# A new prologue order in a fused attention and MLP kernel: norm statistics ahead of applies, all V tiles and wide w1 outputs in the prologue, a bank plan per output

## The chip, the cores and the metric

The kernel runs on one core of a Trainium2 chip. The metric is device time in microseconds (us), the median of three runs. Times named with an engine come from one profiled execution of the kernel before the change.

## The reference, cut to what matters

```python
xn = layernorm(x)                                  # x: 2048 x 448, bf16
qkv = xn @ wqkv                                    # 16 heads of 28
pq, pk = q @ w_phi, k @ w_phi                      # per head, 28 x 28
phi_q = concat(softmax(pq), softmax(-pq))          # 56 features
phi_k = concat(softmax(pk), softmax(-pk))
kv, z = phi_k^T @ v, sum_s(phi_k)
o = (phi_q @ kv) / (phi_q @ z + 1e-6)
A = o @ wo
h = gelu(layernorm(xn) @ w1)                       # four column groups, moved by 1, -1, 2, -2 tokens
x1 = xn + shift(h) @ w2
B = x1 + gelu(layernorm(x1) @ w3) @ w4             # w3: 448 x 1792
out = x + A + B
```

The second layer norm of `xn` is left to the first one in the kernel; `q` and `k` are never formed, because `w_phi` is folded into their weights.

## The kernel before, in words

The 2048 tokens are 16 tiles of 128. The contraction over 448 features uses four overlapping 128-row pieces, held so that every piece has a lower and an upper half of 64 rows; an output needs seven such halves. A matmul on rows 0-63 and one on rows 64-127 run beside each other when their results lie in different PSUM banks, so the code always issues a lower half of one output next to an upper half of another.

A small recorder (`Recorder`) writes every operation into one list in program order. Each engine then executes its own operations in that order, and waits on semaphores where data or a bank demands it. The order written in `play([...])` is therefore the order of each engine's queue. The eight PSUM banks of 512 fp32 columns are assigned by hand. TensorE appears in the profile as PE, VectorE as DVE, ScalarE as ACT, GpSimd as POOL, and SyncE as SP; SP issues most DMAs, and a DMA queued on SP waits behind the ones before it.

The program has three parts.

1. The prologue (lines 361-846, up to 37.76 us). It loads x, normalises it (`ln1`), transposes it into `xnT`, and computes V (`z_v`), the first MLP product with w1 (`z_h`, `z_w1`, `z_rest`) with its GELU, and the folded weights `wpk` and `wpq` (`fold_pair`). `("s", i)` is the statistics of tile i: two VectorE instructions and then the scale on POOL (`ln_scale`: an add and a power, and a negation if POOL is to apply it). `("a", i)` applies it on VectorE, `("p", i)` on POOL. Tiles 0-7 and 12-15 are transposed on TensorE (`xn_T`) with a copy from PSUM; tiles 8-11 go by a DMA transpose on SP (`xn_Td`). `zip_in` issues the lower half of a new output together with the upper half of the one before it. `EV`, `EW` and `rest_out` empty banks: V by a copy, the w1 outputs by a GELU. Column 384 to 447 of w1 is the rest (`z_rest`); its result is transposed by a DMA (`rest_T`), and `h_shift` moves parts of `hT` by the token shifts with six DMAs.
2. The loop of eight passes (lines 858-886, 37.76 to 74.13 us). A pass computes a pair of k tiles, a pair of q pieces, and a side job: either the w2 product of two token tiles (`w2_pair`, added to `xn` on VectorE by `w2_out`) or the V product of two tiles (12 and 13 in pass 1, 14 and 15 in pass 4). From pass 3 it also adds two tiles to the kv product (`kv_tile`, banks 6 and 7). ScalarE takes exponentials of k and q with both signs; `k_norm` sums and inverts on VectorE and multiplies on POOL. The second norm's statistics follow on VectorE (`w2_norm`), and `g_apply` with the DMA transpose `g_T` makes `gT`.
3. The main part (lines 888-947): w3 with GELU (`a(p)` and `b(p)`, halves of a pair), the attention numerators (`N`), the final sums with w4 and wo (`f`), and the stores.

The change touches the x loads (363-374), `xn_T` (492-501), `zip_in` (545-554), the output makers (556-588), `g_apply` (680), `ln1` (797), the two `play` lists (833-846, 920-924) and the pass loop (856-886).

Of the kernel before, what the change touches and what calls it, by code (L numbers as in the profile page):

```python
# [223 lines left out]
def bass_parallel_sum__linear_kernel_hedgehog__mixer_s_mlp__prompt_kernel(  # L224
# [16 lines left out]
    with es:  # L241
# [128 lines left out]
        R.op("ACT", lambda e: e.preload_act_table_set("gelu_apprx_tanh_and_others"), [], [])  # L370
        load_x(6, 2)
        load_x(4, 2, "ACT")
        load_x(12, 4)
        load_x(8, 4, "ACT")
# [117 lines left out]
        def xn_T(i, b, n=1):  # L492
# [6 lines left out]
            for j in range(n):  # L499
                R.act(xnT[:, :, 128 * (i + j):128 * (i + j) + 128].rearrange("p c (h e) -> p c h e", h=2),  # L500
                      t[:, :, 256 * j:256 * j + 256].rearrange("p h (c e) -> p c h e", c=KC), ACT.Copy)
# [40 lines left out]
        KCS = ((0, 1, 2, 3), (0, 2, 3))  # L542
        tail = [None]

        def zip_in(make):
            prev, n4 = tail[0] if tail[0] else (None, True)
            lo = make(LO, KCS[0] if n4 else (0, 1, 3)) if make else []
            hi = prev(HI, KCS[0] if n4 else KCS[1]) if prev else []
            for k in range(max(len(lo), len(hi))):
                for step in (lo[k:k + 1], hi[k:k + 1]):  # L550
                    for mms in step:
                        for out, l, r, first in mms:
                            R.mm(out, l, r, first, False)
            tail[0] = (make, not n4) if make else None

        def z_v(i, b):
            o = banks[b][:, 0:D]

            def make(rows, kcs):
                lo, hi = rows  # L560
                return [[(o, xnT[lo:hi, kc, 128 * i:128 * i + 128], wv[lo:hi, kc, :], rows == LO and n == 0)]
                        for n, kc in enumerate(kcs)]
            return make

        def z_h(t, bs):
            j = 128 * (t % 4)

            def make(rows, kcs):
                lo, hi = rows
                return [[(banks[b][:, j:j + 128], w1[lo:hi, kc, 128 * m:128 * m + 128],  # L570
                          xnT[lo:hi, kc, 128 * t:128 * t + 128], rows == LO and n == 0 and j == 0)
                         for m, b in enumerate(bs)] for n, kc in enumerate(kcs)]
            return make

        def z_w1(g, m, b):
            def make(rows, kcs):
                lo, hi = rows
                return [[(banks[b], w1[lo:hi, kc, 128 * m:128 * m + 128], xnT[lo:hi, kc, 512 * g:512 * g + 512],
                          rows == LO and n == 0)] for n, kc in enumerate(kcs)]
            return make  # L580

        def z_rest(h, b):
            def make(rows, kcs):
                lo, hi = rows
                return [[(banks[b][:, 64 * j:64 * j + 64],
                          xnT[lo:hi, kc, 1024 * h + 128 * j + 2:1024 * h + 128 * j + 130], w1[lo:hi, kc, REST:D],
                          rows == LO and n == 0 and j == 0) for j in range(8)] for n, kc in enumerate(kcs)]
# [92 lines left out]
        def g_apply(i):  # L680
            ln_apply(pool, halves(g_tok[:, i % 4, :]), lap(xn[:, i, :]), mv2, rs2, i)
# [115 lines left out]
        def ln1(*ops):  # L797
            for op, i, *n in ops:
                if op == "s":
                    ln1_stats(i, *(n or (1, 0)))  # L800
                else:
                    ln1_apply(pool if op == "p" else dve, i)

        fps = {(t, m): fold_pair(t, m, b) for t, m, b in ((1, 0, 3), (1, 2, 0), (0, 0, 3), (0, 2, 0))}
# [7 lines left out]
        def ZV(i):  # L812
            return (zip_in, z_v(i, vb[i]))
# [4 lines left out]
        def ZH(t):  # L818
            return (zip_in, z_h(t, (2, 3, 4)))

        def ZW(g, m):
            return (zip_in, z_w1(g, m, gb[g] + m))

        def EW(g, m, n):
            return (w1_out, g, m, gb[g] + m, n)

        def ZR(h, b):
            return (zip_in, z_rest(h, b))

        vb = {0: 5, 1: 6, 2: 7, 3: 5, 4: 6, 5: 7, 6: 5, 7: 6, 8: 5, 9: 6, 10: 3, 11: 4}  # L830
        gb = (2, 0, 0, 5)
        spin(19, 256)
        play([L(("s", 0), ("s", 1), ("a", 0), ("s", 2), ("a", 1), ("s", 3), ("a", 2), ("s", 4), ("a", 3)),
              (xn_T, 0, 0), (spin, 3, 256), (xn_T, 1, 2), ZV(0), ZV(1), (xn_T, 2, 0), ZH(0),
              L(("s", 5), ("a", 4)), EV(0), ZV(2), (xn_T, 3, 0), ZH(1),
              L(("s", 6), ("a", 5)), EV(1), ZV(3), (xn_T, 4, 0), ZH(2),
              L(("s", 7), ("a", 6)), EV(2), ZV(4), (xn_T, 5, 0), EV(3, "DVE"), ZH(3),
              L(("s", 8, 2, 2), ("a", 7)), EV(4), (xn_T, 6, 0), ZV(5), (xn_T, 7, 0), EW(0, 0, 3), ZV(6), ZV(7), EV(5),
              L(("p", 9), ("a", 8)), (xn_Td, 8), (xn_Td, 9), (phi_blocks,),
              ZW(1, 0), ZW(1, 1), EV(6, "ACT", 2), L(("s", 10, 2, 2), ("p", 11), ("a", 10)), (xn_Td, 10), (xn_Td, 11),  # L840
              (load_wT, 0, (1, 2, 3)), ZW(1, 2), ZR(0, 7), EW(1, 0, 3), ZV(8), (rest_out, 0, 7), ZV(9), ZV(10), EV(8, "ACT", 2),
              L(("s", 12, 2, 2), ("p", 13), ("a", 12), ("s", 14, 2, 2), ("p", 15), ("a", 14)), (late_3,), (load_w2,), (rest_T, 0),
# [135 lines left out]
```

## Time and profile before

| item | value |
|---|---|
| time, median of 3 runs (range) | 182.21 us (182.06 to 182.24) |
| profiled execution, time / span | 182.38 / 180.7 us |
| TensorE granted clock | 0.999 |
| TensorE busy | 170.6 us, 94% of the span |
| VectorE / ScalarE / POOL busy | 109.5 / 81.5 / 96.7 us |
| TensorE busy from 6.73 to 37.76 us | 25.68 of 31.03 us |
| TensorE busy from 37.76 to 74.13 us | 35.88 of 36.37 us |
| DMA moved | 16.00 MB, mean 89 GB/s |

A busy share is a mean over parts with different limits, and TensorE's busy time counts a matmul from issue to its modelled end. In the timeline, a note in brackets such as `[0.80 <-DMA xnT<-xn]` is the idle time of the engine just before the row and what ended it. The chain of waits lists start, length, and the work that the end of the run goes back to.

### The profile page before, as it was taken

How to read it: one execution, taken by the hardware profiler on the slowest of the kernel's cores; microseconds unless marked ns; L12 is line 12 of the kernel's file. 1: busy time of each engine (PE TensorE's matmuls, PEld its weight loads, DVE VectorE, ACT ScalarE, POOL GpSimd, SP SyncE). 2: the span in 40 equal slices, each digit the busy share in tenths (PEclk: the TensorE clock that was granted, in tenths of full speed). 3: DMA queues.
4: the chain of work that ended last, by engine and by line, in shares of the span. 5: the costliest groups of instructions: out<-in, count | busy, mean ns of one | idle time of the engine just before them, and what ended most of it. 6: DMA issues, size and time to landing. Idle time of an engine off the chain costs nothing.

```text
span 180.7 us, 5311 instructions
## 1 busy us (share of the span) xinstructions
PE 170.6 (94%) x2323; PEld 91.2 (50%) x2323; DVE 109.5 (61%) x249; ACT 81.5 (45%) x92; POOL 96.7 (54%) x137
## 2 busy tenths in 40 slices
PE   7988977879899999999999999999999999999993
PEld 5566633644455555455455454554555545555551
DVE  5687642478989979834666983651545517474621
ACT  2356646478777977964822422422224213224000
POOL 4655558000779999993065949562350622722740
PEclk9999999999999999999999999999999999999999
DMA  6991346669940114214011241322623120211331
GB/s 162 357 205 22 62 89 160 90 177 335 252 144 4 33 29 76 87 33 83 8 29 33 58 90 31 83 78 60 78 42 83 37 77 0 80 33 29 83 86 44
DMA packets 34743, 16.00 MB, mean 89 GB/s; under 512 B 26016, under 2 KB 34016, under 8 KB 34720
## 3 DMA queue, kind: packets, MB, share of 16 engines
q1 hardware_dynamic: 32944, 14.23, 34.8%
q10 hardware_dynamic: 1776, 1.43, 2.4%
q8 instruction: 18, 0.29, 0.7%
q14 instruction: 5, 0.04, 0.1%
HBM read 7.14 MB, written 1.84 MB: 50 GB/s over the span
## 4 chain that ended last, share of the span: by engine, by line
PE 78%; DVE 9%; DMA 5%; ACT 3%; POOL 1%; issue 1%; ACTq 1%; DVEq 0%
PE banks L203 78%; DMA xtok<-in_A_x_dram 4%; DVE st L215 4%; DVE xn L215 2%; DMA xnT<-xn 1%; ACT hT L211 1%; DVE mv L215 1%; DVE ksum L215 1%; DVE vaug L215 1%; POOL rs L215 1%; ACTq L221 1%; ACT xnT L211 1%; ACT vaug L211 1%; ACT gT L211 0%; DVE rks L215 0%
## 5 line engine op out<-in xcount | busy, mean ns | idle before, releaser
L211 ACT ACTIVATE phik<-banks 128x1024 bf16<-128x1024 f32 (+1 forms) x44 | 42.3, 984 | 63.0 <-PE banks L203 62.9
L203 PE MATMUL banks<-gT,w 64*128 64x512 bf16 x392 | 50.0, 377 | 0.0
L215 DVE TENSOR_TENSOR vaug<-banks,vaug 128x464 f32<-128x464 f32 (+3 forms) x65 | 32.6, 512 | 23.0 <-PE banks L203 21.3
L203 PE MATMUL banks<-w,phik 64*128 64x448 bf16 (+1 forms) x420 | 45.0, 350 | 0.0
L215 POOL TENSOR_TENSOR xnT<-vaug 128x196 bf16<-128x196 f32 (+1 forms) x32 | 18.1, 585 | 46.4 <-DVE vaug L215 46.4
L203 PE MATMUL banks<-wv,xnT 64*128 64x448 bf16 (+1 forms) x218 | 31.8, 350 | 1.2 <-DMA xnT<-xn 1.2
L203 PEld LDWEIGHTS banks<-w,phik 64*128 64x128 bf16 (+1 forms) x420 | 21.7, 94 | 21.2 <-issue 0.4
L215 POOL TENSOR_TENSOR phik<-phik,rks 128x1792 bf16<-128x1792 bf16 x8 | 25.7, 3211 | 10.9 <-DVE rks L215 10.9
L203 PEld LDWEIGHTS banks<-gT,w 64*128 64x128 bf16 x392 | 17.7, 94 | 17.8 <-ACT phik L211 0.4
L203 PEld LDWEIGHTS banks<-wv,xnT 64*128 64x128 bf16 (+1 forms) x218 | 12.1, 94 | 12.2 <-DMA xnT<-xn 2.0
L203 PE MATMUL banks<-xnT,w 64*128 64x128 bf16 (+1 forms) x147 | 16.4, 286 | 0.0
L215 POOL TENSOR_TENSOR vaug<-xn,xtok 128x448 f32<-128x448 bf16 x16 | 16.2, 1032 | 0.2 <-DVE vaug L215 0.2
L215 DVE TENSOR_REDUCE ksum<-phik 128x64 f32<-128x1792 bf16 x8 | 16.1, 2006 | 0.0
L215 DVE RECIPROCAL vaug<-banks 128x16 f32<-128x16 f32 x16 | 4.1, 258 | 17.9 <-PE banks L203 17.9
L203 PE MATMUL banks<-xnT,wpq 64*128 64x512 bf16 x112 | 14.7, 377 | 0.0
L203 PE MATMUL banks<-wpk,xnT 64*128 64x448 bf16 x112 | 13.2, 349 | 1.0 <-ACT gT L211 1.0
L215 DVE TENSOR_TENSOR xn<-banks,xn 128x512 bf16<-128x512 f32 (+1 forms) x16 | 9.2, 616 | 5.6 <-PE banks L203 5.6
L215 POOL TENSOR_SCALAR g_tok<-xn,rs 128x512 bf16<-128x512 bf16 x16 | 12.1, 766 | 0.2
L203 PE MATMUL banks<-w,hT 64*128 64x448 bf16 x96 | 11.7, 350 | 0.5 <-DVE vaug L215 0.5
L215 POOL TENSOR_TENSOR rs<-mv,mhalf 128x1 f32<-128x1 f32 (+2 forms) x16 | 11.3, 705 | 1.3
L215 DVE BATCH_NORM_STATS2 st<-xtok 128x6 f32<-128x448 bf16 x16 | 9.8, 613 | 1.9 <-DMA xtok<-in_A_x_dram 1.9
L211 ACT ACTIVATE xnT<-banks 128x512 bf16<-128x512 bf16 x12 | 6.9, 596 | 7.2 <-PE banks L207 7.2
(66 smaller groups left out, 165.6 us busy)
## 6 DMA issues: line engine op xcount, KB each, us to landing
w<-in_B_w_dram SPq DMA_DIRECT2D x2, 896.0 KB, 6.3
out_dram<-vaug SPq DMA_DIRECT2D x15, 112.0 KB, 1.9
w<-in_B_w_dram SPq DMA_DIRECT2D x1, 1568.0 KB, 10.2
xtok<-in_A_x_dram SPq DMA_DIRECT2D x1, 448.0 KB, 8.2
xtok<-in_A_x_dram ACTq DMA_DIRECT2D x1, 448.0 KB, 8.4
wv<-in_A_wo_dram SPq DMA_DIRECT2D x2, 224.0 KB, 3.9
w<-in_B_w_dram SPq DMA_DIRECT2D x1, 336.0 KB, 3.5
gT<-g_tok SPq DMA_TRANSPOSE x16, 2.5
```

The costliest lines, as they stand in the source:

```text
L203: self.op("PE", lambda e: e.matmul(out, lhsT, rhs, start=start, stop=stop, skip_group_check=True), [out], [lhsT, rhs], tile=self._tile(lhsT))
L211: self.op("ACT", lambda e: e.activation(out, in_, func, **kw), [out], [in_] + aps)
L215: self.op(eng, lambda e: getattr(e, name)(out, *args, **kw), [out], aps)
L221: self.op(eng, lambda e: e.dma_start(out, in_), [out], [in_], dma=True)
```

## The change

Seven things change together.

- x tiles 4 and 5 are loaded one by one on SP's and ScalarE's queues, and the loads of 8-11 and 12-15 keep their queues behind them.
- In the norm, the statistics of tiles 10-11 stand before the applies of 8 and 9, those of 12-13 before 10 and 11, those of 14-15 before 12 and 13.
- `zip_in` merges the two lists of matmuls by columns issued instead of step by step, and takes a list `then`, which is played when the output is whole, that is after the next output's zip.
- w1 group 0 is computed like the other groups, with 512 columns for each of three outputs, in place of four times 128 columns. GELUs take one or two banks instead of three.
- V tiles 12 to 15 are computed at the end of the prologue; the pass loop has w2 jobs in passes 0, 1, 2, 4, 5 and 6 and none in 3 and 7. In passes without a side job the kv tiles come after the first q half.
- Banks are listed per output (`vb`, `gb`) and per pass (`at`: k pair, w2 pair, q pair, each number a pair of banks). The copies of tiles 14 and 15 from PSUM, and the eviction of V4 and V5, go to VectorE; that of V3 goes to ScalarE.
- The second norm's statistics move to fixed passes (`norms`). `g_apply` of tiles 0-3 runs after pass 3; that of tiles 4-7 on VectorE in the main part, after the w2 sum of tile 12, where POOL did it. The kv tiles 14 and 15 come one w3 half later; the load of w3 moves from the middle of the prologue behind `h_shift(1)`.

```diff
         R.op("ACT", lambda e: e.preload_act_table_set("gelu_apprx_tanh_and_others"), [], [])
+        load_x(4, 1)
+        load_x(5, 1, "ACT")
         load_x(6, 2)
-        load_x(4, 2, "ACT")
+        load_x(8, 4, "ACT")
         load_x(12, 4)
-        load_x(8, 4, "ACT")
...
-        def xn_T(i, b, n=1):
+        def xn_T(i, b, n=1, eng="ACT"):
...
+                if eng == "ACT":
+                    R.act(d, a, ACT.Copy)
+                else:
+                    R.ew(dve, "tensor_copy", d, a)
...
+        upper = [[], (), True]
+
+        def zip_in(make, then):
+            high, done, four = upper
+            low = make(LO, (0, 1, 2, 3) if four else (0, 1, 3)) if make else []
+            n, at = [low, high], [0, 200]
+            while n[0] or n[1]:
+                k = int(not n[0] or bool(n[1]) and at[1] < at[0])
+                out, l, r, first = n[k].pop(0)
+                R.mm(out, l, r, first, False)
+                at[k] += max(64, out.shape[-1])
+            play(done)
+            upper[:] = (make(HI, (0, 2, 3) if four else (0, 1, 2, 3)), then, not four) if make else ([], (), True)
...
-        def g_apply(i):
-            ln_apply(pool, halves(g_tok[:, i % 4, :]), lap(xn[:, i, :]), mv2, rs2, i)
+        def g_apply(i, eng=pool):
+            ln_apply(eng, halves(g_tok[:, i % 4, :]), lap(xn[:, i, :]), mv2, rs2, i)
...
-        fps = {(t, m): fold_pair(t, m, b) for t, m, b in ((1, 0, 3), (1, 2, 0), (0, 0, 3), (0, 2, 0))}
+        fps = {(t, m): fold_pair(t, m, b) for t, m, b in ((1, 0, 2), (1, 2, 0), (0, 0, 0), (0, 2, 0))}
...
-        vb = {0: 5, 1: 6, 2: 7, 3: 5, 4: 6, 5: 7, 6: 5, 7: 6, 8: 5, 9: 6, 10: 3, 11: 4}
-        gb = (2, 0, 0, 5)
+        vb = {0: 5, 1: 6, 2: 7, 3: 5, 4: 6, 5: 7, 6: 2, 7: 3, 8: 6, 9: 7, 10: 2, 11: 3, 12: 6, 13: 7, 14: 2, 15: 3}
+        gb = ((2, 3, 4), (0, 1, 4), (4, 6, 7), (5, 2, 3))
         spin(19, 256)
         play([L(("s", 0), ("s", 1), ("a", 0), ("s", 2), ("a", 1), ("s", 3), ("a", 2), ("s", 4), ("a", 3)),
-              (xn_T, 0, 0), (spin, 3, 256), (xn_T, 1, 2), ZV(0), ZV(1), (xn_T, 2, 0), ZH(0),
-              L(("s", 5), ("a", 4)), EV(0), ZV(2), (xn_T, 3, 0), ZH(1),
-              L(("s", 6), ("a", 5)), EV(1), ZV(3), (xn_T, 4, 0), ZH(2),
-              L(("s", 7), ("a", 6)), EV(2), ZV(4), (xn_T, 5, 0), EV(3, "DVE"), ZH(3),
-              L(("s", 8, 2, 2), ("a", 7)), EV(4), (xn_T, 6, 0), ZV(5), (xn_T, 7, 0), EW(0, 0, 3), ZV(6), ZV(7), EV(5),
-              L(("p", 9), ("a", 8)), (xn_Td, 8), (xn_Td, 9), (phi_blocks,),
-              ZW(1, 0), ZW(1, 1), EV(6, "ACT", 2), L(("s", 10, 2, 2), ("p", 11), ("a", 10)), (xn_Td, 10), (xn_Td, 11),
-              (load_wT, 0, (1, 2, 3)), ZW(1, 2), ZR(0, 7), EW(1, 0, 3), ZV(8), (rest_out, 0, 7), ZV(9), ZV(10), EV(8, "ACT", 2),
-              L(("s", 12, 2, 2), ("p", 13), ("a", 12), ("s", 14, 2, 2), ("p", 15), ("a", 14)), (late_3,), (load_w2,), (rest_T, 0),
-              (h_shift, 0), (load_lap, w3, B_w3), ZV(11), ZW(2, 0), EV(10, "ACT", 2), (xn_T, 12, 6, 2), ZW(2, 1), (xn_T, 14, 6, 2), ZW(2, 2),
-              FO(1, 0, 0), FO(1, 0, 1), ZW(3, 0), EW(2, 0, 3), ZW(3, 1), FO(1, 2, 0), FO(1, 2, 1), ZW(3, 2), FO(0, 0, 0),
-              ZR(1, 2), EW(3, 0, 3), FO(0, 0, 1), FO(0, 2, 0), (zip_in, None), (rest_out, 1, 2), FO(0, 2, 1),
-              (rest_T, 1), (h_shift, 1), (load_w4,)])
+              (xn_T, 0, 0), (spin, 3, 256), (xn_T, 1, 2), ZV(0, EV(0)), (xn_T, 2, 0), ZV(1), (xn_T, 3, 2), ZV(2, EV(1)), ZV(3, EV(2)),
+              L(("s", 5), ("a", 4)), (xn_T, 4, 0), ZW(0, 0, EV(3)),
+              L(("s", 6), ("a", 5)), ZW(0, 1), (xn_T, 5, 0), ZW(0, 2, EW(0, 0, 2)),
+              L(("s", 7), ("a", 6)), ZV(4), (xn_T, 6, 0), EW(0, 2, 1),
+              L(("s", 8, 2, 2), ("a", 7)), ZV(5), (xn_T, 7, 0), L(("s", 10, 2, 2), ("p", 9), ("a", 8), (phi_blocks,)), (xn_Td, 8), (xn_Td, 9),
+              ZV(6, EV(4, "DVE", 2)), L(("s", 12, 2, 2), ("p", 11), ("a", 10)), ZV(7), (xn_Td, 10), (xn_Td, 11),
+              ZW(1, 0, EV(6, "ACT", 2)), ZW(1, 1, EW(1, 0, 2)), L(("s", 14, 2, 2)), ZW(1, 2, EW(1, 2, 1)), FO(1, 0, 0), (load_wT, 0, (1, 2, 3)),
+              ZV(8), FO(1, 0, 1), L(("p", 13), ("a", 12), ("p", 15), ("a", 14)), (late_3,), (load_w2,),
+              ZV(9, EV(8, "ACT", 2)), ZR(0, 5, (rest_out, 0, 5), (rest_T, 0), (h_shift, 0)), ZV(10), (xn_T, 12, 0, 2, "ACT"), ZV(11, EV(10, "ACT", 2)),
+              ZW(2, 0), (xn_T, 14, 0, 2, "DVE"), ZW(2, 1), ZW(2, 2, EW(2, 0, 1), EW(2, 1, 2)), FO(1, 2, 0),
+              ZW(3, 0, EW(3, 0, 1)), FO(1, 2, 1), ZW(3, 1), ZW(3, 2, EW(3, 1, 2)), FO(0, 0, 0),
+              ZR(1, 4, (rest_out, 1, 4)), FO(0, 0, 1), ZV(12), ZV(13, EV(12, "ACT", 2)), ZV(14), FO(0, 2, 0),
+              ZV(15, EV(14, "ACT", 2)), FO(0, 2, 1), (zip_in, None, ()),
+              (rest_T, 1), (h_shift, 1), (load_lap, w3, B_w3), (load_w4,)])
...
-        side = [("w", 0), ("v", 12), ("w", 2), ("w", 4), ("v", 14), ("w", 6), ("w", 8), ("w", 10)]
-        g_at = {2: (0,), 3: (1,), 4: (2, 3), 6: (4,), 7: (5,)}
+        side = {0: 0, 1: 2, 2: 4, 4: 6, 5: 8, 6: 10}
+        g_at = {3: (0, 1, 2, 3)}
+        norms = {1: (0, 1), 3: (2, 3), 5: (4,), 6: (5,), 7: (6, 7)}
+        at = {0: (2, 3, 0), 1: (1, 2, 3), 2: (0, 2, 1), 3: (0, None, 2), 4: (1, 0, 2), 5: (1, 0, 2), 6: (1, 0, 2), 7: (1, None, 0)}
         for ps in range(8):
-            k, q = k_pair(2 * ps, 1), q_pair(ps // 2, 2 * (ps % 2), 0)
-            kind, i = side[ps]
-            w = {"w": w2_pair, "v": v_pair}[kind](i, 2)
+            kb, wb, qb = at[ps]
+            k, q = k_pair(2 * ps, kb), q_pair(ps // 2, 2 * (ps % 2), qb)
+            i = side.get(ps)
+            w = w2_pair(i, wb) if i is not None else None
+            kv = [2 * ps - 6, 2 * ps - 5] if ps > 2 else []
             k[0]()
-            if ps > 2:
-                kv_tile(2 * ps - 6)
-                kv_tile(2 * ps - 5)
-            w[0]()
+            if w:
+                for t in kv:
+                    kv_tile(t)
+                w[0]()
             k[1]()
             for s in range(2):
-                k_exp(2 * ps, 1, s)
+                k_exp(2 * ps, kb, s)
             q[0]()
-            w[1]()
-            if kind == "w":
-                w2_out(i, 2)
-            if kind == "v":
-                v_out(i, 4, "DVE" if i == 12 else "ACT")
+            if w:
+                w[1]()
+                w2_out(i, wb)
+            else:
+                for t in kv:
+                    kv_tile(t)
             q[1]()
             for s in range(2):
-                q_exp(2 * ps, 0, s)
-            k_norm(2 * ps)
-            if kind == "w" and i < 8:
-                w2_norm(i)
+                q_exp(2 * ps, qb, s)
+            if ps < 7:
+                k_norm(2 * ps)
+            for j in norms.get(ps, ()):
+                ln_stats(st2, mv2, xn, j)
+                if j % 4 == 3:
+                    ln_scale(mv2, rs2, j - 3, 4, 4)
+            if ps == 7:
+                k_norm(14)
...
-            A(6, 7), G(6, 7),
-            a(0), (wl[12][0],), b(0), a(1), (w2_last, 12), b(1), K(10, 11, 12, 13),
-            a(2), (wl[14][0],), b(2), a(3), K(14, 15), b(3), (kv_copy,),
-            a(4), (w2_last, 14), b(4), a(5), (kv_blocks,), b(5),
+            a(0), (wl[12][0],), b(0), a(1), (w2_last, 12), (lambda: [g_apply(i, dve) for i in (4, 5, 6, 7)],), G(4, 5, 6, 7), b(1), K(10, 11, 12, 13),
+            a(2), (wl[14][0],), b(2), a(3), b(3), a(4), K(14, 15), (kv_copy,), (w2_last, 14), b(4), a(5), (kv_blocks,), b(5),
```

## The prediction

> **What bounds the kernel now.** I read first the 40 slices, then the chain of waits, then the timeline with its idle notes.
>
> ```profile
> PE   7988977879899999999999999999999999999993
> ```
>
> ```profile
> 2.77 6.78 DMA xtok<-in_A_x_dram
> ...
> 16.56 0.71 POOL rs L215
> ...
> 17.58 0.41 DVE xn L215
> ...
> 22.82 2.47 DMA xnT<-xn
> ...
> 37.11 0.60 ACT gT L211
> ...
> 47.62 130.29 PE banks L203 x1706
> ```
>
> The chain has two parts. From 47.62 us on nothing but TensorE work stands in it. Before that it hops between the x load, VectorE's norm chain, POOL's `rs` power, the DMA transposes and ScalarE. So two questions decide: how much TensorE work leaves the late part, and whether the early part takes it in without ending later. The boundary that I use is 37.76, where the first k pair starts. The idle notes name the early waits of TensorE:
>
> ```profile
> 10.78 0.29 PE L207 MATMUL banks<-ident,xn 64*128 64x64 bf16 x8 [0.76 <-DVE xn L215]
> 16.48 0.29 PE L207 MATMUL banks<-ident,xn 64*128 64x64 bf16 x8 [0.59 <-DVE xn L215]
> 24.04 0.93 PE L203 MATMUL banks<-wv,xnT 64*128 64x448 bf16 x8 [0.80 <-DMA xnT<-xn]
> 25.34 0.74 PE L203 MATMUL banks<-wv,xnT 64*128 64x448 bf16 x6 [0.37 <-DMA xnT<-xn]
> 29.14 0.41 PE L207 MATMUL banks<-ident,xn 64*128 64x64 bf16 x16 [1.20 <-ACT xnT L211]
> 33.16 0.68 PE L203 MATMUL banks<-g_tok,hi 64*128 64x84 bf16 x15 [0.48 <-ACT hT L211]
> 37.76 0.93 PE L203 MATMUL banks<-wpk,xnT 64*128 64x448 bf16 x8 [1.02 <-ACT gT L211]
> ```
>
> These are 5.2 us of waits; TensorE is busy 25.68 of the 31.03 us from 6.73 to 37.76, so 5.35 in all. A middle pass (period 60.26 to 64.90, 4.6 us) reads:
>
> ```profile
> 60.26 0.92 PE L203 MATMUL banks<-wpk,xnT 64*128 64x448 bf16 x8
> ...
> 63.00 1.73 ACT L211 ACTIVATE phik<-banks 128x896 bf16<-128x896 f32 x2 [0.24 <-PE banks L203]
> ...
> 64.90 0.92 PE L203 MATMUL banks<-wpk,xnT 64*128 64x448 bf16 x8
> 65.11 1.94 ACT L211 ACTIVATE hi<-banks 128x1024 bf16<-128x1024 f32 x2 [0.38 <-PE banks L203]
> ```
>
> ScalarE has 1.73 + 1.94 = 3.67 us of exponentials in each pass, so TensorE is the bound there, by 0.9 us only.
>
> **The change, part by part.** Unit prices: two 64-row matmuls on different banks run side by side; 14 of 448 columns cost 7 steps. From 8.43, 8.62, 8.81 to 9.00 steps of 448 columns are 0.19 us apart; those of 512 (26.14, 26.37, 26.59) 0.22. An output takes 3.5 steps: 0.67 or 0.76.
>
> *Middle passes.* V12-13 and V14-15 leave passes 1 and 4: 2 x 7 x 0.19 = 2.66 us of TensorE. The 0.49 us wait at 47.62 for V12's eviction goes too. Passes start at 37.76, 41.93, 46.22, 51.04 and so on to 74.13, in all 36.37. After, passes 0 to 2 have a w2 pair and no kv: 3 x 4.17 = 12.5. Passes 4 to 6 keep w2 and kv: 3 x 4.61 = 13.8. Passes 3 and 7 have kv alone: 4.61 - 1.33 = 3.28 each, under ScalarE's 3.67. What is late next? VectorE in pass 1 has the w2 sum 1.16, the k sums 2.01 + 0.55 and two norms 1.5, in all 5.2 against 4.17, so the pass 2 sum comes about 1.2 late and pass 3's q pair, which takes its banks, waits some 0.45. After pass 7 the next pair needs the bank of pass 7's k, whose exponentials end 0.55 later, as ScalarE lags by that. Total 12.5 + 3.7 + 13.8 + 3.3 + 0.55 = 33.9, that is 2.5 less. Bounds: 3.15 less without either stall (2.66 + 0.49), and 0.9 less if both short passes stay at 4.61.
>
> *Norms 4 to 7 of the second layer* go from POOL (0.77 each) to VectorE (4 x 0.41), after the w2 sum of 12. They delay nothing on the path: their transposes issue some 6 us after the pass loop and are read at step a(7), 17 us after it. k_norm(14) now stands behind two norms (1.5 us) on VectorE; its POOL product (3.21) ends some 7.5 us into the main part and the kv tiles 14, 15 now come after a(4), at 11.5. Cost nothing; 4 us of cover, beyond which each us late is a us.
>
> POOL's 0.90 us normalisations at 21.22, 24.48 and 27.75 ran beside VectorE's without a stretch; one at 17.64 took 1.12. The Trainium skill, Advanced Engine Details and Errata, section VectorE Performance Modes, speaks against this move: VectorE's two-port modes and GpSimd block each other on a shared SBUF port. By the rows the POOL product loses nothing; by the rule up to 4 x 0.41 = 1.6 us, still inside the cover.
>
> *Prologue work.* V12-15 add 4 x 0.67 = 2.7 us. w1 group 0 was 4 tiles x 21 matmuls of 128 columns, zipped beside V steps, so 4 x 0.67 = 2.7; it becomes 21 of 512 columns, 3 x 0.76 = 2.3. Net +2.3. The last V15 half runs alone: +0.3.
>
> *x loads.* Tile 4 landed at 9.55 in a 224 KB load on ScalarE's queue, behind w1 (7.6). Now it is a 112 KB load on SP, whose w1 landed at 7.8; the next 224 KB there took 0.8. So about 8.3; bounds 7.9 and 9.55. Tile 3's apply, queued behind tile 4's statistics on VectorE, moves with it: 10.34 becomes 9.1, and TensorE's transpose of tile 3 from 10.78 to 9.5. One more issue on SP (0.45 us) delays tiles 12-15, phi and the weight transposes; all have over 5 us to spare.
>
> *Norm order.* VectorE waited four times for POOL's `rs`, 5.3 us. Statistics of 10-11 now come before the apply of 8, so these waits go. But POOL's apply of 9 falls behind the scale of 10-11, and of 11 behind that of 12-13. My walk on VectorE, with statistics 0.73 and an apply 0.41: from 8.3 each tile takes 1.13, a6 ends at 12.8, the statistics of 8-9 and a7 at 14.6, those of 10-11 at 16.0, a8 and the mask product at 16.8, statistics 12-13 and a10 at 18.6. POOL follows 10-11 with a scale (1.3) and the apply (0.95): 9 ends at 18.5 (before 18.76); then 1.3 + 0.95 again, 11 at 20.7 (before 22.12); plus 2.5 for each transpose, 21.0 and 23.2, on SP's queue 1.2 us apart at least. V9 and V11 are wanted at 23 and 25.7, so the 0.80 and 0.37 us DMA waits go. Behind them on SP are the weight transposes and w2, then h_shift 0, needed from 38 on.
>
> *Banks and evictions.* `then` plays an eviction one zip after the output is whole. The 1536-wide GELUs (1.45 us) become a 1024-wide (1.02) and a 512-wide (0.6): 0.2 us more ScalarE work per group. Late next on my walk: the tile 6 copy behind a GELU makes the tile 7 transpose wait 0.65, V7 0.25 for its xnT, fold 1 0.35 for the eviction of V6-7. With tile 2 (0.25) and tile 3 (0.9) that is 2.4. The old waits of 1.20, 0.48 and 1.02 on ScalarE go: V11 and a w1 output now stand between the transposes of 12-13 and of 14-15, the folds' banks hold no GELU's input, and the k pair of pass 0 takes banks whose last reader is the rest GELU of four outputs earlier.
>
> *Half folds.* Two fold halves back to back cost a wait on the own bank:
>
> ```profile
> 30.61 0.19 PEld L203 LDWEIGHTS banks<-g_tok,hi 64*128 64x128 bf16 x8 [0.20 <-PE banks L203]
> ```
>
> Zips now part them, -0.2 at two or more places; in passes 3 and 7 k's halves become neighbours, +0.2 twice: nothing. The Trainium skill, TensorEngine Tiling (Array Packing), section Restrictions and Gotchas, says that different row tiles cannot access one PSUM bank simultaneously; if each meeting cost a whole matmul (0.35), both sides would still cancel.
>
> *Prologue sum.* By the account of waits: work +2.3 + 0.3, waits 2.4 + 0.2 instead of 5.35: about -0.2. By my walk, step after step from 9.5: V2-3, w1 group 0, V4-7 and four transposes with their waits end at 18.7; group 1 and half a fold at 21.8; V8-9, the other half, rest 0, V10, transposes 12-13 and V11 at 26.5; groups 2 and 3, three half folds and transposes 14-15 at 32.9; rest 1, V12-15 and three half folds at 38.6, +0.4 for the slow 64-column rest steps (1.24 us measured from 21.26): 39.0, +1.2. The two differ in the small waits at each zip, which I cannot see. I take +0.6, in the middle; bounds -0.8 (all ScalarE waits gone) and +3.5 (six more copies 0.6 us late).
>
> **Sum.** -2.5 + 0.6 = -1.9. The profiled run took 182.38 (span 180.7 and 1.7 around it), giving 180.5; it stands 0.17 above the median, so 180.3.
>
> **Rivals.**
> 1. *ScalarE convoy, slower.* Copies, evictions and GELUs share one in-order queue (17.87 us busy up to 37.76, some 0.9 more after: two V evictions of 0.92 and 0.2 per GELU group come, three copies of 0.54 to 0.6 net go to VectorE), and `then` delays them. Its place is tiles 5 to 8, where two GELUs and four copies follow each other. If the prologue ends 3.2 later, the loop's 2.5 gain is lost: 182.9; it decides from +2.5 on. For it: ScalarE ended three of the waits shown. Against: over 10 us of the prologue stay free on ScalarE. 0.22.
> 2. *Tile 4 lands no earlier.* Both queues carry the same bytes; +1.2 to the early chain: 181.5. Against: SP's faster landing. 0.13.
> 3. *Short passes do not shrink*, VectorE or ScalarE holding them at 4.6: +1.6, 181.9. For it: VectorE's 5.2 in pass 1. 0.10.
> 4. *All waits go*, prologue at 37.0: 179.0. For it: VectorE's 5.3 us of waits for `rs` are free then. Against: the copies behind GELUs on my walk. 0.18.
>
> **Numbers.** Likeliest 0.37, own range 179.6 to 181.1. A measurement of this kernel tells about 0.2% (0.36 us) from no change. Faster: 0.37 + 0.18 + most of rivals 2 and half of 3 = 0.70, less 0.02 for unknown mishaps, 0.68; same 0.08; slower 0.24. The range 178.6 to 183.2 takes in rivals 4 and 1 and leaves out one in ten at each end.
>
> **What would show it.** Right: transpose of tile 3 at 9.5, no VectorE wait on `rs`, k pair of pass 0 between 37.5 and 39.2, passes 3 and 7 of about 3.5 us, and 34 us from there to a(0). Wrong: idle notes naming ScalarE `xnT` or `hT` of over 4 us in sum before the loop, tile 4 landing near 9.5, or passes 3 and 7 at 4.6.

## The result and the profile after

The changed kernel takes 180.94 us (median of 20 runs, 19 of them between 179.81 and 182.42), the kernel before 182.2 in the same comparison: a ratio of 0.9938, 95% interval 0.9911 to 0.9964. In a later comparison on one chip it was 182.15 against 182.39, a ratio of 0.9952 (0.9923 to 0.998). The medians take in every run and the ratios leave out the slow ones: one of 254.23 us at a granted clock of 0.661 in the first comparison, two of 183.0 and 183.1 in the later one. The gain is real and small, 0.5 to 0.6%, and the spread of the new kernel's 19 runs (2.6 us) is wider than that of the old one (1.6). They fall into two groups: nine with a mean clock near 0.99, median 182.0, and ten with 0.998 to 1.00, median 180.5. The profiled execution belongs to the first group. It took 181.97 us, 0.41 less than the profiled one before, with a span of 180.2.

The 40 slices of the changed kernel, first TensorE's busy tenths, then the granted clock:

```profile
PE   7979979999999999999799999999999999999993
PEclk9969999999999999999999999999999999999999
```

The clock is not constant any more: slice 2 (9 to 13.5 us) shows 6. The windows view names the place. Its columns are the stretch, its length, then busy time (and instructions) of TensorE, its weight load, VectorE, ScalarE and POOL, the granted clock, the DMA share and GB/s. The clock changes here in steps of 3.41 us, so the stretches are chosen to fit:

```profile
3.57:6.98 3.41, 3.31 (x30) 1.88 (x28) 2.90 (x9) 1.05 (x2) 2.03 (x6) 1.00 1.02 310
6.99:10.40 3.41, 1.99 (x32) 0.77 (x29) 2.30 (x7) 1.73 (x3) 1.54 (x5) 1.00 1.08 353
10.40:13.81 3.41, 3.41 (x29) 2.06 (x25) 3.31 (x10) 1.54 (x3) 2.68 (x7) 0.50 1.29 142
13.81:17.22 3.41, 3.41 (x46) 2.02 (x44) 3.27 (x11) 2.69 (x6) 1.82 (x6) 1.00 0.25 51
```

After a window in which TensorE was busy for 1.99 of 3.41 us comes one at half clock, full of work. It costs about half its length, 1.7 us. The idle notes of TensorE show what emptied the window before it, and the pace behind it:

```profile
10.12 0.29 PE L207 MATMUL banks<-ident,xn 64*128 64x64 bf16 x8 [1.32 <-DVE xn L215]
10.25 2.90 PE L203 MATMUL banks<-wv,xnT 64*128 64x448 bf16 x14
...
27.07 0.41 PE L207 MATMUL banks<-ident,xn 64*128 64x64 bf16 x16 [1.22 <-DVE xn L215]
...
88.78 1.04 PE L203 MATMUL banks<-gT,w 64*128 64x512 bf16 x8 [1.08 <-ACT phik L211]
```

From 6 us on these three are all waits above a quarter of a microsecond. Of the seven of before six are gone; the one before tile 3's transpose, 0.76 at 10.78, is still there and has grown to 1.32. The fourteen V matmuls at 10.25 take 2.90 us. In the chain of waits the end now goes back to TensorE from 29.26 us, not 47.62, with the exponentials of pass 7 and one wait at 88.78 in between:

```profile
2.70 6.20 DMA xtok<-in_A_x_dram
...
24.49 2.52 DVE xn L215
...
29.26 22.70 PE banks L203 x283
52.01 16.58 PE banks L203 x274
68.61 1.94 ACT hi L211 x2
70.55 1.63 ACT phik L211 x2
72.22 8.58 PE banks L203 x136
80.84 6.88 PE banks L203 x106
87.74 1.03 ACT phik L211
88.78 88.73 PE banks L203 x1060
```

One link in it is a VectorE instruction far longer than its kind: 2.52 us for an apply. The wait at 88.78 is at a(7), the first step that reads `gT` of tiles 4 to 7. The trace names the gelu that ended just then, but in e1 below the same step does not wait for that gelu, and in the second trace of this kernel the wait ends with the transposes of `gT`. So the transposes are the likelier cause, and they follow four VectorE applies of 4.25 us in sum. VectorE's and POOL's timelines lie side by side at both places:

```profile
24.41 2.91 DVE L215 TENSOR_SCALAR xn<-xtok,mv,rs 128x512 bf16<-128x512 bf16 x2
...
77.55 4.25 DVE L215 TENSOR_SCALAR g_tok<-xn,mv,rs 128x512 bf16<-128x512 bf16 x4 [0.25 <-POOL rs L215]
```

```profile
24.35 0.31 POOL L215 MEMSET wpq<- 128x256 bf16 x1
24.60 1.81 POOL L426 MEMSET phik<- 128x2048 bf16 x1
26.34 0.53 POOL L215 MEMSET kvq<- 128x512 bf16 x1
...
77.47 3.21 POOL L215 TENSOR_TENSOR phik<-phik,rks 128x1792 bf16<-128x1792 bf16 x1
```

An apply takes 0.41 us elsewhere. Beside POOL's memsets the first of the two takes 2.60 and ends at 27.01, just behind the last of the three (26.87). Beside POOL's product the first of the four takes 3.28 and ends at 80.83, just behind it (80.68).

So by profile against profile: the first k pair starts at 37.78 (before 37.76), the loop takes 34.44 instead of 36.37, and the main part, from a(0) to the last matmul's end, takes 105.31 instead of 103.81. The sum is +0.0 - 1.9 + 1.5 = -0.4, as timed. The prologue paid for four more V tiles in spite of a half-clock window; the loop gained; the main part gave most of it back. Of its 1.5 us the wait at a(7) is 1.08; e1's main part, without that wait, takes 104.0, so 0.2 goes with the change itself, and the rest is not explained.

### The profile page after: what moved, and what is told of

Read it like the earlier page. It is cut to its first block, busy times and chain, and to the rows that moved or that the text cites. A ratio compares the mean times of both kernels' runs of the same rounds, so it can differ in the third digit from the quotient of the medians.

```text
span 180.2 us, 5192 instructions
## 1 busy us (share of the span) xinstructions
PE 171.9 (95%) x2260; PEld 93.8 (52%) x2260; DVE 115.5 (64%) x254; ACT 82.0 (45%) x94; POOL 92.9 (52%) x133
## 3 DMA queue, kind: packets, MB, share of 16 engines
q10 hardware_dynamic: 1648, 1.32, 2.3%
## 4 chain that ended last, share of the span: by engine, by line
PE 87%; ACT 4%; DMA 3%; DVE 3%; SPq 1%; issue 0%; DVEq 0%
PE banks L203 86%; DMA xtok<-in_A_x_dram 3%; DVE xn L215 2%; ACT phik L211 1%; ACT hi L211 1%; SPq L221 1%; PE banks L207 1%; ACT hT L211 1%; DVE wpk L215 1%; ACT xnT L211 1%; DVE st L215 0%; DVE vaug L215 0%; DVEq L176 0%; DVE mv L215 0%
## 5 line engine op out<-in xcount | busy, mean ns | idle before, releaser
L203 PE MATMUL banks<-wv,xnT 64*128 64x448 bf16 (+1 forms) x218 | 32.7, 365 | 0.1
L203 PEld LDWEIGHTS banks<-wv,xnT 64*128 64x128 bf16 (+1 forms) x218 | 12.8, 97 | 9.7 <-PE banks L203 1.4
L203 PE MATMUL banks<-xnT,wpq 64*128 64x512 bf16 x112 | 16.2, 376 | 0.0
L203 PE MATMUL banks<-wpk,xnT 64*128 64x448 bf16 x112 | 15.5, 350 | 0.1
L203 PE MATMUL banks<-xnT,w 64*128 64x512 bf16 x84 | 13.9, 384 | 0.0
L203 PE MATMUL banks<-w,hT 64*128 64x448 bf16 x96 | 13.6, 349 | 0.0
L203 PEld LDWEIGHTS banks<-wpk,xnT 64*128 64x128 bf16 x112 | 6.5, 94 | 5.5 <-PE banks L203 1.0
L215 DVE BATCH_NORM_STATS2 st<-xn 128x6 f32<-128x448 bf16 x16 | 9.3, 582 | 0.0
```

The costliest lines, as they stand in the source:

```text
L203: self.op("PE", lambda e: e.matmul(out, lhsT, rhs, start=start, stop=stop, skip_group_check=True), [out], [lhsT, rhs], tile=self._tile(lhsT))
L215: self.op(eng, lambda e: getattr(e, name)(out, *args, **kw), [out], aps)
```

## The experiments

Theory A: the prologue loses about 1.7 us to a clock window that TensorE's wait before tile 3's transpose opens. The 128-column w1 matmuls stood there before. Theory B: the main losses are VectorE's two blockings by POOL. Rivals: the norm order, the x loads or the V tiles' place carry the result.

**e1_spin: keep TensorE busy before tile 3.** Ten unused 512-column matmuls, in pairs on two banks, go in front of the transposes.

```diff
-  (xn_T, 2, 0), ZV(1), (xn_T, 3, 2),
+  (xn_T, 2, 0), ZV(1), (spin2, 5), (xn_T, 3, 2),
```

> The changed kernel with five pairs of unused 512-column matmuls (1.1 us) in TensorE's idle time before the transpose of tile 3; nothing else differs, and what they write is overwritten. Theory, the clock gate follows TensorE's idle time: the granted clock is 1.00 in every run, the times fall together near 180.3 us, and from 10 to 15 us the granted clock reads 1.00 in place of 0.66; the V pairs after the transpose take 0.19 us each. Rival, the half clock comes at random or from elsewhere: about half of the runs still show a mean clock of 0.99 and some 182 us. Second rival, the low clock costs nothing because ScalarE or the DMAs bound this stretch: the clock is 1.00 and the median stays at 180.9.

Measured: 178.63 us (178.05 to 180.46), ratio 0.9794 (0.9759 to 0.983). Work that computes nothing makes the kernel some 2 us faster than the changed one, which is more than the theory had. Five of the six runs have a mean clock of 1.00; the sixth, 180.46, has 0.99, so the clock was not at 1.00 in every run as expected. TensorE's timeline of this run:

```profile
9.44 0.28 PE L207 MATMUL banks<-ident,xn 64*128 64x64 bf16 x8
9.56 1.72 PE L203 MATMUL banks<-wv,xnT 64*128 64x448 bf16 x14
...
23.90 0.35 PE L203 MATMUL banks<-wv,xnT 64*128 64x448 bf16 x1 [1.25 <-DMA xnT<-xn]
```

The V matmuls take 1.72 instead of 2.90, and the first k pair starts at 35.53, 2.25 earlier. Some 0.7 of that is the x load, which landed earlier here (the transpose is at 9.44, not 10.12). That much can be chance: tile 4's statistics start between 7.96 (here) and 9.62 in the eleven traces with the new loads. From a(0) to the end the span is 1.3 us shorter, 106.7 against 108.0, and a(7) has no wait. A new wait of 1.25 us appears, V10 for its DMA transpose. The wait before the transpose of tiles 12 and 13 is gone. In the changed kernel the apply of 12 came late, behind a VectorE copy of TensorE's fold result (23.40 to 24.49), and met the memsets. Here it starts at 22.16, ahead of them, and takes 0.68; the one that POOL blocks is the apply of 14 (3.3 us, to 26.09), and TensorE comes to tile 14 only at 26.53.

**e7_zh: real work in the gap.** w1 group 0 as two outputs of 256 columns, the first between the transposes of tiles 2 and 3.

```diff
-  ZV(1), (xn_T, 3, 2), ZV(2, EV(1)), ZV(3, EV(2)), ... (xn_T, 4, 0), ZW(0, 0, EV(3)),
+  ZV(1), ZH(0), (xn_T, 3, 0), ZV(2, EV(1)), ZV(3, EV(2)), ... (xn_T, 4, 0), ZH(2, EV(3), (w1_out, 0, 0, 2, 2)),
```

> The changed kernel with w1 group 0 in two parts of 256 columns: that of tiles 0 and 1 stands before the transpose of tile 3, that of tiles 2 and 3 after the transpose of tile 4. Work replaces idle time. Theory: the clock stays at 1.00 in every run, and the 1.1 us of work that fills the gap is gained besides, 179.2 to 179.8 us; two parts cost up to 0.2 us more in matmuls of half the width. Rival, 512 columns are what pays: 180.5 or more.

Measured: 178.97 us (178.28 to 179.42), ratio 0.98 (0.9774 to 0.9825), a little below the expected range. The granted clock was 1.00 in all six runs. Useful matmuls do what the unused ones do. New waits: 0.90 at 16.04 for a ScalarE copy and 1.44 for V10's DMA transpose. With e1, this is the version that beats both kernels, by 2% against the one before.

**e8_after: the changed kernel again**, for a second trace.

> The changed kernel itself, beside the next three on one chip. Theory, the half clock in the V steps after the transpose of tile 3 is in nearly every run of it, whatever the mean clock says: 1.5 to 2 us above the run with the filled idle time (178.6), so 180.2 to 181.2, and the 14 V matmuls take some 2.9 us in its trace. Rival, the filled run gained by an earlier x tile 4: the V matmuls take 1.7 us and tile 4 lands near 8.9.

Measured: 182.15 us (180.14 to 183.1). Same pattern: a wait of 1.31 before tile 3, clock 0.50 from 11.22 to 14.63, a wait of 1.24 before tiles 12 and 13, and at a(7) one of 1.33, here named `DMA gT<-g_tok`. The median is above the expected 180.2 to 181.2. Of the twelve runs the eight with a mean clock of 0.981 to 0.991 take 181.8 to 183.1, the four at 0.999 or 1.00 take 180.1 to 181.3.

**e2_nospin: without the three warming matmuls** behind the first transpose.

```diff
-  (xn_T, 0, 0), (spin, 3, 256), (xn_T, 1, 2),
+  (xn_T, 0, 0), (xn_T, 1, 2),
```

> The changed kernel without the three warming matmuls after the first transpose, so that TensorE is idle some 0.8 us more between 6 and 10 us. Theory, the gate follows idle time: nearly every run shows the half clock, mean clock 0.99 or lower, median 181.9 or more. Rival, the half clock comes at random: about half of the runs at 180.4 and half at 182, as in the changed kernel.

Measured: 181.58 us (179.87 to 182.7), ratio 0.9946: no difference from the changed kernel that these runs can tell. Its windows view and timeline disagree:

```profile
9.90:13.30 3.40, 3.40 (x33) 2.05 (x29) 3.30 (x11) 1.69 (x4) 2.67 (x6) 1.00 1.04 174
```

```profile
9.91 3.03 PE L203 MATMUL banks<-wv,xnT 64*128 64x448 bf16 x14
```

Fourteen matmuls in 3.03 us are at half pace, though the clock column says 1.00. The record of the clock starts only behind them, at 13.4 us (in the other traces between 4.3 and 7.1), and the V matmuls before 9.9 us are no faster (six take 1.33 us at 8.57, 0.73 in the changed kernel). So this is not a dip after full pace: full pace came late. A mean clock of 1.00 does not prove full pace early on; the pace of the matmuls does. At a(7) this trace waits 0.62 us, again for `DMA gT<-g_tok`.

**e12_gap: the same gap in the kernel before**, by moving each of the 128-column w1 outputs behind the next transpose.

```diff
-  (xn_T, 2, 0), ZH(0), ... ZV(2), (xn_T, 3, 0), ZH(1),
+  (xn_T, 2, 0), ... ZV(2), (xn_T, 3, 0), ZH(0),
```

> The kernel before, with each of the four 128-column w1 outputs of group 0 one transpose later, so that nothing but V work stands between the transposes of tiles 2 and 3 and TensorE idles some 1.4 us instead of 0.76 before tile 3. Theory (an idle time of over a microsecond there lets the clock fall): the window 10 to 15 us shows a granted clock under 0.8, the 448-column V matmuls after tile 3 stand 0.38 us apart instead of 0.19, and the time is 1.2 to 2 us above the kernel before, 183.4 to 184.2. Rival (the fall belongs to something else in the changed kernel, such as its wide w1 matmuls or its evictions): the clock stays at 1.00, V steps stay at 0.19, and only the 0.7 us of displaced work shows, 182.2 to 182.9.

Measured: 182.22 us (181.91 to 183.16), ratio 0.9996 (0.9975 to 1.0016), with a mean clock of 0.999 or 1.00 in all ten runs. As I put it, theory A missed: taking the w1 matmuls away was not enough. The trace shows why this was no clean copy of the gap:

```profile
9.38 0.93 PE L203 MATMUL banks<-wv,xnT 64*128 64x448 bf16 x8 [0.69 <-ACT xnT L211]
10.62 0.29 PE L207 MATMUL banks<-ident,xn 64*128 64x64 bf16 x8 [0.31 <-DVE xn L215]
```

```profile
6.89:10.30 3.41, 2.72 (x32) 1.34 (x26) 1.75 (x6) 1.63 (x3) 1.14 (x3) 1.00 1.10 370
...
27.37:30.78 3.41, 2.15 (x46) 1.15 (x44) 0.41 (x1) 2.56 (x5) 3.31 (x5) 1.00 0.57 131
```

Here V2 precedes tile 3's transpose and splits the idle time into 0.69 and 0.31, and the window stays at 2.72 us busy. Its second row, 2.15 busy, is not followed by half clock either. Put together over the traces: windows with 1.67, 1.99 and 2.06 us busy were followed by half clock; of those with 2.15 to 2.22, three were (2.18, 2.19, 2.22) and four were not (2.15, 2.17, 2.19, 2.21); above that none. The busy time decides at the low end; what decides between 2.15 and 2.22 stays open.

**e3_late: the memsets behind the applies**, on top of e1.

```diff
-  R.ew(pool, "memset", wpad, 0.0)
+  R.op(pool, lambda e: e.memset(wpad, 0.0), [wpad], [xn[:, NT - 2, :]])
```

> As the run with the filled idle time, and POOL's three memsets of late_3 wait until the applies of tiles 12 and 14 are done. Theory, a POOL memset holds VectorE's tensor_scalar: the apply of 12 takes 0.4 us instead of 2.6, the transposes of 12 and 13 start near 25.4 (clock 1.00) without the 1.2 us wait, and the time falls by 1.0 to 1.2 us against the run with the filled idle time. Rival, the long apply waits for the V eviction or the weight cast and not for POOL: it stays at 2.6 us and the time does not move.

Measured: 178.75 us (178.22 to 179.06), ratio 0.9787 (0.9764 to 0.9809). The tile's answer shows the applies (minimum, median, maximum in ns), first of e1, then of this run:

```profile
L215 DVE TENSOR_SCALAR xn<-xtok,mv,rs x12: 379/411/3318, 5.0 to 22.8; 128x512 bf16<-128x512 bf16 x12
```

```profile
L215 DVE TENSOR_SCALAR xn<-xtok,mv,rs x12: 381/412/865, 5.2 to 23.1; 128x512 bf16<-128x512 bf16 x12
```

The blocking is shown to be POOL's: 3.3 us becomes 0.87 when the memsets wait. But V10's wait, 1.16 us, stays, and the time with it; the fall of 1.0 to 1.2 us did not come. It could not: in e1 the blocked apply was that of 14, and TensorE did not wait for it.

**e4_kn: POOL's last product behind VectorE's four second-norm applies**, on top of e1. `k_norm(14)` does its sums where it did, and returns the product as a step for later.

```diff
-  k_norm(14)
+  k_last = k_norm(14)
...
+  (lambda: [g_apply(i, dve) for i in (4, 5, 6, 7)],), (k_last,),
```

> As the run with the filled idle time, and POOL's product of the last k_norm waits until VectorE's four applies of tiles 4 to 7 are done. Theory, a POOL product holds VectorE's tensor_scalar: the four take 1.6 us instead of 4.25, their transposes start 2.5 us earlier and the wait before a(7), 0.2 to 1.1 us, goes; the kv tiles 14 and 15 come up to 0.5 late. Time 178.0 to 178.8. Rival, the applies wait for the scale on POOL or are slow by their shape: they stay at 4.25.

Measured: 179.17 us (178.76 to 180.57), ratio 0.9833 (0.9801 to 0.9866), not the expected 178.0 to 178.8.

```profile
77.43 1.38 DVE L215 TENSOR_SCALAR g_tok<-xn,mv,rs 128x512 bf16<-128x512 bf16 x4 [0.28 <-POOL rs L215]
```

The four applies fall from 4.25 to 1.38 us, and there is no wait at a(7). But e1 and e7 have none there either, with applies of 4.25: the blocking alone does not make the wait. In e1 the `gT` transposes took 5.13 us from the first issue, in the changed kernel 6.50. The wait stands in the three traces of the changed kernel and of e2, where the gap is not filled (1.08, 1.33 and, in e2, 0.62), and in none of the nine with a filled one. Why the transposes are slower there is not shown.

**e5_all: both**, on top of e1.

```diff
+  R.op(pool, lambda e: e.memset(wpad, 0.0), [wpad], [xn[:, NT - 2, :]])
...
+  (lambda: [g_apply(i, dve) for i in (4, 5, 6, 7)],), (k_last,),
```

> The filled kernel with both of VectorE's blockings by POOL taken away: the memsets wait for the applies of 12 and 14, and POOL's last product waits for the second norm's four applies. Theory: the applies take 0.4 to 0.9 us, there is no wait at a(7), and the time stays within 0.3 of the filled kernel, 178.3 to 178.9, because V10's wait for its DMA transpose takes the place of the one in the prologue. Rival: the two add up to what the main part lost, 177.2 to 178.0.

Measured: 179.18 us (178.67 to 179.66, four runs), ratio 0.982 (0.9777 to 0.9864). The runs at full mean clock are at 178.67 and 178.78, the two others at 179.57 and 179.66. Nothing is gained over e1: theory B falls as an account of the time in the filled kernel. Its first part holds where TensorE runs late. The profiled runs of e4 (180.57) and of this version (179.57) both have a half-clock window and transpose tile 3 at 11.66. In e4 the memsets meet the apply of 12, and TensorE waits 1.10 us before tiles 12 and 13; here it does not wait, and the first k pair starts at 36.65 instead of 37.63. This run shows the clock once more, at another place:

```profile
4.97:8.38 3.41, 2.19 (x34) 0.94 (x33) 2.54 (x8) 1.20 (x2) 2.06 (x7) 1.00 0.99 318
8.38:11.80 3.42, 3.42 (x30) 1.36 (x30) 2.78 (x8) 1.14 (x2) 2.15 (x5) 0.50 1.38 278
11.80:15.21 3.41, 3.41 (x53) 1.99 (x51) 3.31 (x11) 2.61 (x5) 2.04 (x6) 1.00 0.75 130
```

The filler stands before tile 3, and here the thin window lies before tile 2: several short waits for x tiles between 5 and 8.4 us. Where the 3.41 us grid falls differs from run to run (one of its windows begins between 4.3 and 7.1 us in these traces), so the same code meets it or not.

**e6_xload: the old x loads**, on top of e1, with ten pairs of filler.

```diff
-  load_x(4, 1); load_x(5, 1, "ACT"); load_x(6, 2); load_x(8, 4, "ACT"); load_x(12, 4)
+  load_x(6, 2); load_x(4, 2, "ACT"); load_x(12, 4); load_x(8, 4, "ACT")
```

> The changed kernel with ten pairs of unused 512-column matmuls before tile 3's transpose (so that TensorE stays busy up to it) and with the x loads of the kernel before. Theory (the prediction's x load step): tile 4 lands at 9.2 to 9.6 instead of 7.9, the transpose of tile 3 comes at 10.6 to 10.9 instead of 9.44, and the time is about 1.2 above the filled kernel's 178.6, 179.5 to 180.1. Rival (V10's wait for its DMA transpose or another later wait absorbs it): 178.5 to 179.0.

Measured: 180.15 us (179.49 to 181.95), ratio 0.9862 (0.9815 to 0.9909). Tile 4's statistics start at 9.97 against 7.96 in e1's trace and 8.93 in the changed kernel's. Over all traces they start between 9.42 and 9.97 with the old loads (three traces), between 7.96 and 9.62 with the new (eleven, median 8.6). The three runs with a mean clock of 0.999 or 1.00 have a median of 179.94, e1's five of 178.53: the step is worth 1.4, or 1.7 when each is set against the kernel before on its own chip. The profiled run caught a half-clock window in which its longer filler ran at half pace, so its later times are not used.

**e10_stats: the statistics back behind the applies**, on top of e1.

```diff
-  L(("s", 10, 2, 2), ("p", 9), ("a", 8), (phi_blocks,)), ... L(("s", 12, 2, 2), ("p", 11), ("a", 10))
+  L(("p", 9), ("a", 8), (phi_blocks,)), ... L(("s", 10, 2, 2), ("p", 11), ("a", 10))
```

> As the run with the filled idle time, but the statistics of 10-11, 12-13 and 14-15 go back behind the applies of 8 to 12, one step later each. The prediction's terms: VectorE waits 1.2 to 1.4 us for POOL's rs three times, POOL's apply of 9 comes 1.3 earlier, those of 11 to 15 later. Theory: V10 now waits for the DMA transposes anyway, and the apply of 9 comes earlier, so most of it is hidden; +0.2 to +0.8 us, 178.8 to 179.4. Rival, the norm order carries the gain: +2 us or more, 180.6.

Measured: 179.89 us (179.61 to 180.98), ratio 0.9873 (0.9845 to 0.9901), 1.3 above e1 and between the theory and its rival. VectorE waits for POOL again:

```profile
15.90 0.41 DVE L215 TENSOR_SCALAR xn<-xtok,mv,rs 128x512 bf16<-128x512 bf16 x1 [1.16 <-POOL rs L215]
19.48 0.41 DVE L215 TENSOR_SCALAR xn<-xtok,mv,rs 128x512 bf16<-128x512 bf16 x1 [1.38 <-POOL rs L215]
23.75 0.41 DVE L215 TENSOR_SCALAR xn<-xtok,mv,rs 128x512 bf16<-128x512 bf16 x1 [0.40 <-POOL rs L215]
27.02 0.41 DVE L215 TENSOR_SCALAR xn<-xtok,mv,rs 128x512 bf16<-128x512 bf16 x1 [1.38 <-POOL rs L215]
```

Of these 4.3 us, 1.3 reach the end. The norm order is a part of the gain in its own right.

**e9_vloop and e11_vloop: V12 to V15 back in the loop**, as side jobs of passes 3 and 7, on top of e1. In e9 the load of wo overwrote the tile of wv in pass 5, so its V14 and V15 multiply wo's weights and wait for that load (1.39 us at 73.64). e11 moves the load behind pass 7; the last pair of lines in the diff is e11's alone.

```diff
-  FO(0, 0, 1), ZV(12), ZV(13, EV(12, "ACT", 2)), ZV(14), FO(0, 2, 0), ZV(15, EV(14, "ACT", 2)), FO(0, 2, 1),
+  FO(0, 0, 1), FO(0, 2, 0), (zip_in, None, ()), FO(0, 2, 1),
...
+  v = {3: (12, 1), 7: (14, 2)}.get(ps)
-  if ps == 5: load_lap(wo, A_wo)
+  if ps == 7: load_lap(wo, A_wo)
```

> As the run with the filled idle time, but V12-13 and V14-15 go back into the loop as side jobs of passes 3 and 7, the two without one; everything else of the change stays. The prediction's terms: the prologue gives back 2.7 + 0.3 us, the two passes take 1.33 each, less their two stalls of 0.45 and 0.55, so the loop is 1.7 longer and the time 1.3 shorter, 177.3. Theory: h_shift 0 is issued near 29.6 and lands near 39, and V12-15 are what TensorE does meanwhile; without them the w2 pair of pass 0 waits for hT, and the time is 178.6 or more. Rival, ScalarE's extra evictions in the loop cost: a wait on ScalarE at pass 4 instead, same time or more.

> The filled kernel with V12-13 and V14-15 back as side jobs of passes 3 and 7, this time with the load of wo, which overwrites wv, after pass 7, so that pass 7 multiplies wv and waits for no load. Theory (V12 to 15 in the prologue are cover for the token shift's DMAs and the folds' copies): the first k pair still starts at 36.2 to 37.0 with waits on DVE wpq and DMA hT, the loop is 38.5 to 39.5, and the time is 1.2 to 1.6 below the earlier run with the load in pass 5: 183.3 to 183.8. Rival (the earlier run's loss was that load's wait and what came behind it): 179.5 to 181.0.

Measured: e9 184.93 us (183.96 to 185.97), ratio 1.0136 (1.0103 to 1.017); e11 184.07 (182.99 to 184.65), ratio 1.0082 (1.0046 to 1.0118). e11 is 5 us slower than e1 with the same matmuls. Its idle notes from the end of the prologue on:

```profile
33.70 0.21 PE L203 MATMUL banks<-g_tok,hi 64*128 64x84 bf16 x1 [0.79 <-DVE wpq L215]
34.30 0.29 PE L203 MATMUL banks<-g_tok,hi 48*128 48x56 bf16 x7 [0.39 <-DVE wpq L215]
36.20 1.67 PE L203 MATMUL banks<-wpk,xnT 64*128 64x448 bf16 x8 [0.58 <-ACT gT L211]
...
52.30 0.93 PE L203 MATMUL banks<-wv,xnT 64*128 64x448 bf16 x8 [0.83 <-ACT eq_lo L211]
56.43 0.93 PE L203 MATMUL banks<-wpk,xnT 64*128 64x448 bf16 x8 [0.55 <-ACT vaug L211]
72.48 0.93 PE L203 MATMUL banks<-wv,xnT 64*128 64x448 bf16 x8 [0.82 <-ACT hi L211]
```

Without V12 to V15 the first k pair starts no earlier: 26.0 us after tile 3's transpose (10.20 to 36.20), against 26.1 in e1 (9.44 to 35.53). The folds' copies and gelu, until then covered, become waits of 1.8 us. The first pass, 36.20 to 41.75, also runs partly at half clock, behind a window that these waits leave thin (2.22 us busy, 32.22 to 35.63). In the loop passes 3 and 7 take 6.33 and 5.61 instead of 3.55 and 3.81, 4.6 more for 2.7 of work; V's output now takes banks that the exponentials still read. That last part belongs to where I put V, not to the kernel before, which had another bank plan.

## Why the prediction was right, point by point

The forecast, 180.3, lies 0.6 below the measured 180.94, and faster was right. But that closeness is in part luck, since errors cancel. Between the two profiles the prologue came out 0.6 better than forecast, the loop 0.6 worse, and the main part, which had no term, 1.5 worse.

- **Middle passes.** Predicted 33.9, measured 34.44, and 34.45 in e1. Passes 3 and 7 take 3.55 and 3.81, as the sum with its two stalls had it (3.28 + 0.45 and 3.28 + 0.55). Passes 4 to 6 are 4.61, 4.61 and 4.62. The term mis-sized is that of passes 0 to 2, 13.24 instead of 12.5: V15's last matmuls still run beside the first k pair, so pass 0 is 4.57 instead of 4.17, and pass 2 is 4.51. There the w2 pair's first weight load waits 0.28 us for VectorE's sum of pass 1, a stall that I had looked for only in pass 3.
- **Short passes do not shrink** (rival 3): not so.
- **Norms 4 to 7 on VectorE.** This failed. The prediction read POOL's applies, 0.90 and 1.12 us, as running without a stretch, and costed the move at nothing. Such an apply takes 0.77 in the changed kernel, and 0.90 to 1.12 again in e10, where the old order returns, so those rows did show the two engines holding each other up. The step looked at what POOL would lose; VectorE lost: 4 x 0.41 became 4.25. The transposes were issued 8.6 us after the loop instead of 6, a(7) wanted them after 15.5 instead of 17, and so the 4 us of cover were gone. The wait at a(7) is 1.08 us, 1.33 in the second trace. The Trainium skill, Advanced Engine Details and Errata, section VectorE Performance Modes, states that GpSimd and VectorE's two-port instructions block each other, and the traces agree that the two engines do. The prediction's estimate from that rule was 1.6 us; measured are 2.6 in the main part and 2.1 at the applies of 12 and 14. Later runs limit what the blocking decides: e1 has it too, and no wait at a(7). By these numbers it took the cover, and the 1.4 us that the transposes lost then came through.
- **Prologue work and sum.** Predicted +0.6, with bounds of -0.8 to +3.5. Measured +0.0 to the start of the first k pair, +0.4 if V15's rest is counted to it. This lands within the range for a reason the text did not have: it holds a loss of about 1.7 us to the clock and a wait of 1.22 for a blocked apply, so all else came out near -2.5. My walk was too slow; the account of waits (-0.2) was nearer, and e1, at 35.53, shows what the rest could do. The bank plan and the merge by columns have no run of their own.
- **x loads.** Predicted landing at 8.3, measured 8.90 in the profiled run and 7.93 in e1. The transpose of tile 3 came at 10.12 and 9.44 instead of 9.5. e6 puts the step at 1.4 to 1.7 us; rival 2 is refuted in the median, though in single traces (9.40 in e8, 9.62 in e9) tile 4 came hardly earlier than before.
- **Norm order.** All four waits for `rs` are gone, the DMA waits of V9 and V11 too. e10 prices this at 1.3 us, which the text left inside its sum. What is late next my walk did not name: in the changed kernel the apply of 12, in e1 V10.
- **Banks and evictions.** The ScalarE waits of 1.20, 0.48 and 1.02 went, as said. Of the new small waits (0.65, 0.25, 0.35) none is above 0.25 in the idle notes. The convoy (rival 1) did not come.
- **All waits go** (rival 4, 179.0): e1 and e7 reach its time, 178.6 and 179.0, though V10's wait is left. The changed kernel misses it by the clock window and by a(7).
- **What the text lacked** is the clock. It took the old clock of 0.999 as given, and costed the removal of the 128-column matmuls before tile 3 as work saved. They also kept TensorE busy. The Trainium skill, TensorE: Matmul & The Clock Gate, Part 1: The HAM clock gate, tells of a free-running window of 3413 ns and of half rate after an idle one. The traces agree on the 3.41 us and on the half. They differ on idle: a window that was busy for 1.99 of its 3.41 us was enough.

Between theory A and the rest the runs leave this. That filling the gap saves about 2 us is shown twice, by e1 and by e7. Between the two profiles it is 3.5 us: 0.7 from tile 4's landing, 1.6 from tile 3's transpose to the first k pair, which is the half-clock window (2.90 against 1.72 us for one V output pair) with what it delays, and 1.3 from a(0) on, mostly a(7)'s wait. In the medians these are not separated. The changed kernel's runs near a mean clock of 0.99 are 1.5 us above those at 0.998 to 1.00, which is the price of a window in the record. But the latter, at 180.5 and, in e8, 180.8, are still 2.0 to 2.2 us above e1's five at 178.5, and a(7)'s wait of 1.1 to 1.3 us covers only a part. e2's trace shows that such a mean can hide an early half pace; whether it does in those runs has no trace and stays open.

## What to carry to other kernels

Before taking small matmuls out of a place where TensorE waits, count its busy time in the 3.4 us around that place: here 2.2 us or less risked a window at half clock, worth 1.7 us, and matmuls that compute nothing paid for themselves. When work moves to VectorE, look for the long POOL instruction that will run beside it, and price the move by that instruction's length. And when a wait goes, ask which one stands next: in the filled kernel two clean repairs of the blockings were worth nothing, since V10's transfer was late anyway and a(7) no longer waited, while with TensorE late by a window one of them was worth 1.0 us.

## What the runs showed of the hardware

- The granted clock fell to 0.50 for exactly one window of 3.41 us, then rose again, in every trace that had it. The grid's start differs from run to run, and with it whether a thin stretch falls into one window.
- A bf16 apply of 128 x 512 on VectorE, 0.41 us elsewhere, lasted 2.6 us beside three POOL memsets in a row (0.31, 1.81 and 0.53 us), 3.3 us in e1 beside a POOL apply and the same memsets, and 3.3 us beside a POOL product of 3.21. Each time it ended some 0.15 us behind the last of them. Delaying POOL brought it back to 0.38 to 0.87.
- POOL's apply took 0.77 us in the changed kernel, and 0.90 to 1.12 started beside VectorE's in the kernel before and in e10: the loss is on both sides.
